# Sliding-window attention beside a long convolution on one core: projections and turns in row halves, bf16 taps through ScalarE, and a new written-out order

## The chip, the cores and the metric

The kernel runs on one core of a Trainium2 chip. Its engines are TensorE (PE: matrix products into PSUM, with weight loads shown as PEld), VectorE (DVE), ScalarE (ACT), GpSimd (POOL), and SyncE (SP), which here only issues DMAs. Each engine works through its own queue in the order in which the program was written for it. The metric is device microseconds of one launch. The kernel before takes 209.3 us (median of 3 runs, 209.15 to 209.7).

## The reference

Two independent parts with S = 2048 rows and D = 576 columns, bf16, written side by side into one output of 2048 x 1152.

```
# part A: attention, 32 heads of 18, each row looks at 8 rows: itself, 2, 4, ... 14 rows back
qkv = x @ wqkv                                   # 2048 x 1728
logits[s, w] = q[s] . k[s - 2w] * 18**-0.5       # masked where s - 2w < 0
a = (softmax(logits) @ v_window) @ wo
# part B: gated long convolution, each of the 576 channels by itself
k_shift[s] = sum over l < 4 of k[s - l] * shift_k[l]
kv = k_shift * v
y = irfft(rfft(kv, 2S) * rfft(ssm_k, 2S))[:S] + kv * ssm_D
out = concat([a, q * y], axis=-1)
```

## The kernel before, in words

Part A. x arrives transposed (channels on partitions), four quarters of 512 rows: three by DMA transposes (`load_x`), the quarter of rows 512 to 1023 by `turn_x`, which loads it straight (`xn`) and turns it on TensorE with 20 identity matmuls (`nx0`, `nx1`, `nx2`; evictions `nx0e` and so on). `heat` gives TensorE 13 matmuls on zeros ahead of that. `project(comp, ct, hh)` computes q, k or v (comp 0, 1, 2) for 128 of the columns (ct 0 to 3; ct 4 is the last 64) and 1024 rows (hh). It sums over 576 = 4 x 128 + 64 channels: four full matmuls for each 512 rows, and one "tail" of 64 channels, which stands in one half of the array's rows. So each q or k unit is eight matmuls of 128x128 and two tails of 64x128; each v unit is sixteen of 128x64 (every ninth column, so that heads land where they are wanted) and four tails of 64x64. ScalarE evicts each unit (`p...e`, L445, L450). `logits` (L473 on VectorE, L481 on TensorE) and `softmax` follow, then `weigh` (L725, L739) and `output` (L790).

Part B. `taps` computes k_shift as matmuls with diagonal 64x64 weights (L535), and VectorE multiplies the PSUM result by v (L543; one of each pair of instructions reads both of its operands backwards, with step -1). `fold` turns kv to rows on partitions and makes sums and differences of mirrored rows, with `F1` = [I, I] and `F2` = [I, -I] (L556, L557, L570, L571). `load_filter` mirrors the filter by a matmul with an exchange matrix `JS`, and a second matmul with `EA` or `EB` adds the one edge row (L605, L606). `filter_spectrum`, `odd_spectrum` and `x_spectrum` are cosine and sine transforms with tables TK and TX, which come from integer multiplications on VectorE (`tab...`, L274, L276) of two iotas that GpSimd writes (`const0`), and ScalarE's Sin. For each of the four output blocks j and three column groups t, `products` (L835) multiplies spectra, `sums` (L859) adds them up in 32x32 matmuls, `inverse` (L892) turns them back, `gate` multiplies by q. In block 3 `carry` adds what block 2 left over, by four identity matmuls of 384 columns for each t (L846), ahead of `sums`; in blocks 1 and 2 a DMA that adds in flight does it (`d{j}{t}`, on GpSimd's queue).

What sets the order: the functions only make a list of named operations. `ORDER`, a table of base-36 numbers, gives the order in which they are written out, and with each a slot: which quarter of PSUM an operation takes, or, for `move`, which engine does it (slot 1 is VectorE, otherwise ScalarE). Within each engine that order is the queue. Names in the texts: `p101` is project(1, 0, 1), `L013` a logits matmul, `a0` to `a3` the weighing matmuls, `Z201` a sum, `i10` an inverse.

`const0` to `const3` fill GpSimd's tables: `const0` the iotas, `const1` the identity, `const3` the head selectors EH (twelve selects) and the pads, `const2` the sign variants of the identity and the 32x32 ones.

## Time and profile before

| | |
|---|---|
| median of 3 runs | 209.3 us (209.15, 209.3, 209.7) |
| span of the profiled execution | 207.9 us (the page gives this span and no time of that execution beside it; the median is 1.4 us above it) |
| busy: PE, DVE, ACT, POOL | 197.1, 177.1, 142.3, 56.9 us |
| TensorE instructions | 3173 matmuls, 3173 weight loads |
| mean DMA rate | 154 GB/s, 32.09 MB |

A row of the groups reads: line, engine, operation, out<-in, shapes, count | busy us of the group, mean ns of one | idle time of the engine ahead of them and who ended it. Busy is the union over the group, so overlapping instructions count once: on TensorE the mean of one is its latency, several run at once, and throughput is read from the starts of the first and the last of a row of them. A stretch of the windows view gives for each engine its busy us there.

### The profile page before, as it was taken

What the parts mean: (1) busy time and instruction counts of PE and PEld (TensorE: products, weight loads), DVE (VectorE), ACT (ScalarE), POOL (GpSimd) and SP (SyncE); (2) the same over time, 40 slices, a digit from 0 to 9 for tenths busy, and PEclk for the clock granted to TensorE, in tenths of its full rate; (3) what the DMA queues carried; (4) which work ended last, traced back from release to release, by engine and by line L of the source; (5) the groups of instructions that cost most, each with busy time, mean ns of one, the idle gap of its engine ahead of it and who ended that gap; (6) DMA issues with size and microseconds to landing.
All of it is one profiled execution on the core that took longest, in us unless ns stands there. A gap on an engine that the chain in (4) does not pass through costs nothing.

```text
span 207.9 us, 7147 instructions
## 1 busy us (share of the span) xinstructions
PE 197.1 (95%) x3173; PEld 133.1 (64%) x3173; DVE 177.1 (85%) x147; ACT 142.3 (68%) x173; POOL 56.9 (27%) x105
## 2 busy tenths in 40 slices
PE   7899999999999999999998969998999999999991
PEld 2433334554644557778787857685689878787690
DVE  7306899769878898889999998999999998999963
ACT  2525479875977715578989857988898767665541
POOL 7981033001041195010899900000003020110000
PEclk9999999999999999999999999999999999999998
DMA  6998979999999959945880263106345865749834
GB/s 170 225 223 150 199 150 194 162 185 130 116 180 213 203 99 188 184 110 120 181 221 6 42 162 103 32 3 199 126 167 114 230 177 141 184 131 255 260 126 114
DMA packets 55254, 32.09 MB, mean 154 GB/s; under 512 B 42032, under 2 KB 52408, under 8 KB 55224
## 3 DMA queue, kind: packets, MB, share of 16 engines
q1 hardware_dynamic: 52520, 26.33, 57.2%
q0 software_dynamic: 2176, 4.73, 13.3%
q10 hardware_dynamic: 528, 0.59, 1.0%
q8 instruction: 24, 0.39, 0.8%
q14 instruction: 6, 0.05, 0.1%
HBM read 5.90 MB, written 4.72 MB: 51 GB/s over the span
## 4 chain that ended last, share of the span: by engine, by line
PE 84%; DMA 5%; ACT 5%; DVE 2%; SPq 1%; issue 1%; DVEq 0%
PE PS L419 24%; PE PS L790 10%; PE PS L892 7%; PE PS L859 6%; PE PS L660 5%; PE PS L481 5%; PE PS L429 4%; PE PS L535 4%; PE PS L645 3%; PE PS L739 3%; ACT mem L745 3%; DMA mem<-in_A_wqkv_dram 3%; DMA mem<-in_A_wo_dram 2%; PE PS L581 2%; PE PS L921 2%; DVE mem L725 2%
## 5 line engine op out<-in xcount | busy, mean ns | idle before, releaser
L419 PE MATMUL PS<-mem 128*64 128x512 bf16 (+1 forms) x304 | 51.5, 385 | 0.7 <-DMA mem<-in_A_wqkv_dram 0.7
L473 DVE TENSOR_TENSOR mem<-mem 128x4096 bf16<-128x4096 bf16 (+1 forms) x20 | 40.7, 2074 | 7.0 <-PE PS L481 4.2
L725 DVE TENSOR_TENSOR mem<-mem 128x4096 bf16<-128x4096 bf16 x18 | 40.3, 2290 | 1.9 <-PE PS L739 1.2
L419 PEld LDWEIGHTS <-mem 128*64 128x64 bf16 (+1 forms) x304 | 26.6, 144 | 22.1 <-issue 6.8
L835 DVE TENSOR_TENSOR mem<-mem 128x4608 bf16<-128x4608 bf16 (+3 forms) x21 | 38.4, 1867 | 1.6 <-PE PS L859 1.4
L190 ACT ACTIVATE mem<-PS 128x768 bf16<-128x768 f32 (+1 forms) x49 | 35.2, 761 | 5.8 <-PE PS L582 2.7
L445 ACT ACTIVATE mem<-PS 128x1024 bf16<-128x1024 f32 x24 | 24.2, 1022 | 19.6 <-PE PS L419 11.8
L193 POOL DMA_DIRECT2D mem<-mem x16 | 13.8, 1009 | 80.9 <-ACT mem L870 45.3
L402 POOL COPY mem<-mem 64x16 bf16<-64x16 bf16 x24 | 18.9, 788 | 22.4 <-ACT mem L445 21.6
L790 PE MATMUL PS<-mem 128*128 128x288 bf16 x160 | 21.9, 286 | 0.9 <-DMA mem<-in_A_wo_dram 0.9
L660 PE MATMUL PS<-mem 128*128 128x192 bf16 x192 | 18.7, 246 | 0.2 <-ACT mem L874 0.2
L790 PEld LDWEIGHTS <-mem 128*128 128x128 bf16 x160 | 15.3, 98 | 5.2 <-DMA mem<-in_A_wo_dram 1.2
L892 PE MATMUL PS<-mem 128*128 128x192 bf16 x192 | 17.7, 246 | 0.1
L660 PEld LDWEIGHTS <-mem 128*128 128x128 bf16 x192 | 15.9, 98 | 1.6 <-issue 1.2
L892 PEld LDWEIGHTS <-mem 128*128 128x128 bf16 x192 | 15.8, 98 | 1.2 <-issue 1.0
L859 PE MATMUL PS<-mem 32*32 32x384 bf16 x960 | 13.9, 325 | 1.3 <-ACT mem L745 0.9
L795 ACT ACTIVATE mem<-PS 128x576 bf16<-128x576 f32 x16 | 10.4, 651 | 5.4 <-PE PS L790 4.5
L543 DVE TENSOR_TENSOR mem<-PS,mem 128x512 bf16<-128x512 f32 (+1 forms) x20 | 11.5, 630 | 2.5 <-PE PS L535 2.4
L859 PEld LDWEIGHTS <-mem 32*32 32x32 bf16 x960 | 9.5, 88 | 5.0 <-issue 2.2
L896 ACT ACTIVATE mem<-PS 128x768 bf16<-128x768 f32 x12 | 9.6, 810 | 4.4 <-PE PS L892 4.4
L870 ACT ACTIVATE mem<-PS 128x1536 bf16<-128x1536 f32 x6 | 8.7, 1451 | 5.4 <-PE PS L859 5.2
L429 PE MATMUL PS<-mem 64*64 64x512 bf16 (+1 forms) x76 | 11.7, 412 | 0.0
(113 smaller groups left out, 285.7 us busy)
## 6 DMA issues: line engine op xcount, KB each, us to landing
mem<-mem SPq DMA_DIRECT2D x16, 256.0 KB, 4.2
mem<-mem POOLq DMA_DIRECT2D x8, 288.0 KB, 5.5
out_dram<-mem SPq DMA_DIRECT2D x16, 144.0 KB, 2.9
mem<-in_B_q_dram SPq DMA_DIRECT2D x4, 576.0 KB, 4.4
mem<-mem SPq DMA_DIRECT2D x6, 384.0 KB, 4.1
mem<-mem POOLq DMA_DIRECT2D x6, 384.0 KB, 4.1
mem<-in_A_wqkv_dram SPq DMA_DIRECT2D x3, 576.0 KB, 5.1
out_dram<-mem SPq DMA_DIRECT2D x6, 288.0 KB, 3.5
```

The lines of the kernel that those rows point to most:

```text
L190: act(o, i, ACT.Copy, scale=scale)
L402: nc.gpsimd.tensor_copy(M1(to, PAD)[64 * a:64 * a + 64], M1(frm, PAD)[64 * a:64 * a + 64])
L419: mm(box.ps[p, jp, :], ws[a % len(ws)], xT(kb, 1024 * hh + 512 * (jp ^ a), 512), start=first and kb == 0, stop=last and kb == 3, tile_posi ...
L429: mm(box.ps[p, jp, :], ws[a % len(ws)][64 * r:64 * r + 64], xT(4, 1024 * hh + 512 * r, 512)[64 * r:64 * r + 64], start=first, stop=not fir ...
L445: op(nm + "e", lambda: act(M(o + pad, [[KH if comp == 2 else 512, 2], [1, 512]]), box.ps, ACT.Copy), box, free=True)
L473: op(f"l{hh}{ug}{ct}", lambda prod=prod, nt=nt, qo=qo, ko=ko, ug=ug: tt(M(prod, [[nt, 4], [1, nt]]), M(qo, [[0, 4], [1, nt]]), M(ko + 2 + ...
L660: mm(box.ps[:, gi // 2, TH * (gi % 2):TH * (gi % 2) + TH], M1(TX + 1024 * c + 512 * pm + 128 * gi, 128), M1(AB + 2304 * i + 1152 * c + 576 ...
L725: op(f"w{n}{ct}", lambda: tt(M(P, [[2048, 2], [256, W], [1, 256]]), M(XB[n], [[2048, 2], [256, W], [1, 256]]), M(vo + 2, [[256, 2], [2, W] ...
L790: mm(box.ps[:, h, 0:HD], M1(lhs, 128), M1(rhs, HD), start=(i == 0), stop=(i == 4))
L835: tt(M(pr + 768 * k, [[2304, n], [768, m], [1, 768]]), M(BS + i * SPB + o + PL * k, [[SPB, n], [PL, m], [1, 768]]), M(VS + (3 - j + i) * S ...
L859: mm(view(box.ps[32 * c:32 * c + 32], box.step * (r // 2) + 512 * (r % 2), [[TH, 2], [1, TH]]), I32S[w][32 * r:32 * r + 32], M(pr + src + ...
L892: mm(box.ps[:, pm, TH * c:TH * c + TH], M1(TI + 512 * sl + 256 * pm + 128 * c, 128), M1((YT if j else YRS[0]) + 1536 * t + 768 * pm + TH * ...
```

## The change

1. `project`: except for q of the first 1024 rows, every 128-channel product is split in two of 64 channels, in the upper and the lower half of the array's rows (`quadrants`). The two halves of the rows work at the same time on different PSUM banks, and in a second phase they swap banks; the tail is a matmul like all others. The operation is in two parts (`p...q`, then `p...`), and between them `between` puts an empty instruction (`p...n`) on the engine that the slot names (0 GpSimd, 1 VectorE, 2 ScalarE, 3 SyncE): it waits for the first part, and the second waits for it. The two 64-column units (ct 4) of q and k, and of v's two halves, become one operation (`project_last`).
2. `fold` turns 64 channels at a time with 64-row weights and 128 moving columns, two at once; each eviction is in two, by ScalarE or VectorE (`move`).
3. `taps`: ScalarE copies PSUM to bf16 (20 copies), VectorE then multiplies SBUF by SBUF (`t...m`).
4. `load_filter`: the second matmul is gone; GpSimd writes the edge row (`hg..`, 1 x 576) after the eviction.
5. Block 3, t 0 and 1: no `carry`; a DMA that adds in flight (`d30`, `d31`) after the eviction, ahead of `inverse`.
6. `gate` of blocks 0 to 2: ScalarE copies the mirrored half out of PSUM (`g..e`), one VectorE multiplication of 1152 columns in place of two of 576 that read PSUM.
7. Weights of q and k arrive in two column parts (256 and 320 columns); `nx0e` to VectorE, `nx2e` to ScalarE.
8. `ORDER` is another table (760 operations in place of 676).

```diff
 ORDER = """
-1o u 26 0 10 20 6 86 8u 1c 90 c 1u 7c 8c 6o 6u 2p 70 2c 96 2u 32 19 36 2i 1i 76 b0 66 3o bx 3u 3c 3i
...
+u 2c 6 o c 0 7o 16 1c 1i 26 1u 1o 12 96 9c 9i 8o 2l 38 2v 4c 20 46 30 3o 3u 3i 40 5u 5o 66 60 7u 3c
...
     def mirrors():
         mirror(M1(JS, 128), 1.0, -128)
-        for t, f in ((EA, float(np.sqrt(0.5))), (EB, 1.0)):
-            nc.gpsimd.memset(M1(t, 128), 0.0)
-            nc.gpsimd.memset(M1(t, 1)[0:1], f)
...
-        dma(f"w{comp}", M(b, [[D, 4], [1, D]]),
-            A_wqkv[0:512, comp * D:(comp + 1) * D].rearrange("(kb p) a -> p kb a", p=128), eng)
+        for c0, c1 in ((0, 256), (256, D)) if comp < 2 else ((0, D),):
+            dma(f"w{comp}" + "b" * (c0 > 0), M(b + c0, [[D, 4], [1, c1 - c0]]),
+                A_wqkv[0:512, comp * D + c0:comp * D + c1].rearrange("(kb p) a -> p kb a", p=128), eng)
...
-            op(f"nx{u}e", (lambda box=box, dst=dst: act(dst, box.ps, ACT.Copy)) if u < 2 else
-               (lambda box=box, dst=dst: nc.vector.tensor_copy(dst, box.ps[:, 0:1, :])), box, free=True)
+            op(f"nx{u}e", lambda box=box, dst=dst, n=len(kbs): move(dst, box.ps[:, 0:n, :]), box, free=True)
...
+    def phase(box, ph, runs):
+        first = None
+        for n in range(max(len(run) for run in runs)):
+            for run in runs:
+                if n < len(run):
+                    o, w, i, pos = run[n]
+                    ins = mm(o, w, i, start=ph == 0 and n == 0, stop=ph == 1 and n == len(run) - 1, tile_position=pos)
+                    first = first or ins
+        if ph:
+            tc.add_manual_dep(first.ins, box.half.ins.name, AFTER, reason="the other half of the rows sums here too")
+        box.half = ins
+
+    def between(nm, box):
+        def fence():
+            nop = (nc.gpsimd, nc.vector, nc.scalar, nc.sync)[Op.slot].nop()
+            tc.add_manual_dep(nop.ins, box.half.ins.name, AFTER, reason="behind the first halves")
+            box.half = nop
+        op(nm + "n", fence, box)
+
+    def quadrants(box, ph, parts):
+        runs = []
+        for lo, cols, r1, x0, bank, tail in parts:
+            r = r1 ^ ph
+            h = slice(64 * r, 64 * r + 64)
+            runs.append([])
+            for kb in [0, 1, 2, 3] + [4] * (tail == r):
+                w = cols(kb)
+                m = w.ap[-1][1]
+                runs[-1].append((box.ps[lo:lo + m, bank, :], w[h], xT(kb, x0, 512)[h], (64 * r, lo)))
+        phase(box, ph, sorted(runs, key=lambda run: run[0][3]))
...
+            op(nm + "q", lambda: quadrants(box, 0, parts), box, 1)
+            between(nm, box)
+            op(nm, lambda: quadrants(box, 1, parts), box)
...
-                op(f"t{pr}{n}{'hl'[lo]}", lambda box=box, s=s, b=b, lo=lo, n=n, nb=nb: tt(
-                    M(KV + 1024 * n + 256 * lo, [[512, nb], [1, 256]]), view(box.ps, b, s), M(VT + 1024 * n + b, s),
-                    ALU.mult), box, free=bool(lo))
+                op(nm, lambda box=box, s=s, b=b, kv=kv: act(kv, view(box.ps, b, s), ACT.Copy), box, free=bool(lo))
+                op(nm + "m", lambda s=s, b=b, n=n, kv=kv: tt(kv, kv, M(VT + 1024 * n + b, s), ALU.mult))
 
     def fold(pr):
+        def turn(box, h, b, mt, to):
+            k = slice(64 * h, 64 * h + 64)
+            o = view(box.ps, 512 * h + to, [[256, 2], [1, 64]])
+            return [(o, w[k], M(ID + i + 64 * h, [[128, 2], [1, 64]])[k], i == 128, h)
+                    for w, i in ((M1(b + 128 * mt, 128), 128), (M1(b + 256 + 128 * mt, 128), 0))]
...
-                    mm(o, M1(JS, 128), M1(a + D * (1 - c) + HD * h, HD), start=True, stop=False)
-                    mm(o, M1(EB if c else EA, 128), M1(a + D * c + HD * h, HD), start=False, stop=True)
+                    mm(o, M1(JS, 128), M1(a + D * (1 - c) + HD * h, HD), start=True, stop=True)
...
+            op(f"hg{d}{c}", lambda c=c: edge(M1(FT + 2 * D * d + D * c, D)[0:1], M1(a + D * c, D)[0:1], c))
...
+            elif j == 3 and first:
+                dma(f"d{j}{t}", M(YT + 1536 * t, [[768, 2], [1, 768]]), M(YRS[2] + 1536 * t + 768, [[-768, 2], [1, 768]]),
+                    nc.gpsimd, accum_op=ALU.add)
...
+            if n == D:
+                op(f"{nm}e{e // w}", lambda box=box, e=e: act(M(y + e, [[D, 2], [1, w]]), box.ps[:, :, 0:w], ACT.Copy), box,
+                   free=True)
...
+        if n == D:
+            op(nm + "l", lambda: tt(M(qb, d), M(y, d), M(qb, d), ALU.mult))
```

Three places where the order moves. The first is GpSimd's queue at the start of the program. Before, the iotas of `const0` (L209 to L212) stand first, then `const1` (L218 to L222), then the twelve selects of `const3`:

```order
L209 IOTA rp_i 128x2
L210 IOTA rp_i 128x2
L212 IOTA mem 128x128 x4
L218 MEMSET mem 128x128
L219 AFFINE_SELECT mem<-mem 128x128 [waits Pool_49]
L222 COPY mem<-mem 64x64 [waits Pool_49]
L222 COPY mem<-mem 64x64
L232 AFFINE_SELECT mem<-mem 128x32 [waits Pool_49]
L234 AFFINE_SELECT mem<-mem 128x32 [waits Pool_49]
```

In the changed kernel the same queue begins with `const1` (L224 to L228) and `const2` (L261 to L268); the selects of `const3` (L237 to L245) follow, and the iotas (L215 to L218) come last, ahead of the two small DMAs of `sh`:

```order
L225 AFFINE_SELECT mem<-mem 128x128 [waits Pool_49]
L228 COPY mem<-mem 64x64 [waits Pool_49]
L228 COPY mem<-mem 64x64
L261 COPY mem<-mem 128x128 [waits Pool_49]
L262 TENSOR_SCALAR mem<-mem 128x128
...
L245 AFFINE_SELECT maskb<-maskb 32x128 [waits Pool_49]
L215 IOTA rp_i 128x2
L216 IOTA rp_i 128x2
L218 IOTA mem 128x128 x4
L199 DMA sh<-in_B_shift_k_dram 128x4
```

The iotas moved from the first place to behind all other constants.

The second is VectorE's queue from the program's start. Before, the table multiplications (L274, L276) wait for GpSimd's iotas, and the eviction of `nx2` (L322) stands behind nine of them:

```order
L334 MEMSET mem 128x256
L207 MEMSET pib 128x1
L213 CAST rp<-rp_i 128x4 [waits Pool_49]
L274 TENSOR_SCALAR mem<-mem,rp 128x512 [waits DVE_49,Pool_49]
L274 TENSOR_SCALAR mem<-mem,rp 128x512 x6
L276 TENSOR_SCALAR mem<-mem 128x1024 [waits DVE_49]
L276 TENSOR_SCALAR mem<-mem 128x1024
L322 CAST mem<-PS 128x512 [waits PE_49]
L350 TENSOR_TENSOR mem<-mem,sh 128x1280 [waits DMASW1_49,DMASW0_49,Pool_49]
```

In the changed kernel L277 and L279 are those multiplications, and L194 is `nx0e`, the eviction of the first two 128-channel groups of the turned x (1024 columns):

```order
L337 MEMSET mem 128x256
L213 MEMSET pib 128x1
L219 CAST rp<-rp_i 128x4 [waits Pool_49]
L277 TENSOR_SCALAR mem<-mem,rp 128x512 [waits DVE_49,Pool_49]
L277 TENSOR_SCALAR mem<-mem,rp 128x512 x2
L279 TENSOR_SCALAR mem<-mem 128x1024 [waits DVE_49]
L277 TENSOR_SCALAR mem<-mem,rp 128x512 x2
L194 TENSOR_SCALAR mem<-PS 128x2x512 [waits PE_49]
```

`nx0e` is new in this queue and stands behind the cast and six table multiplications, of which the first waits for the iotas.

The third is ScalarE's queue around the first taps. Before, two projections' evictions (L445, L450), the tables' evictions (L380), the logits' (L487) and the filters' (L609, L190) follow each other:

```order
L380 ACTIVATE mem<-PS 128x1024 [waits PE_49] x2
L487 ACTIVATE mem<-PS 128x1024 [waits PE_49]
L450 ACTIVATE mem<-PS 128x512 [waits PE_49]
L609 ACTIVATE mem<-PS 128x576 [waits DMAHW0_49,DVE_49,PE_49]
L487 ACTIVATE mem<-PS 128x1024 [waits PE_49]
L609 ACTIVATE mem<-PS 128x576 [waits PE_49] x2
```

In the changed kernel the taps' copies (L583) stand between the same kinds of evictions (L383, L525, L660):

```order
L383 ACTIVATE mem<-PS 128x1024 [waits PE_49]
L525 ACTIVATE mem<-PS 128x1024 [waits PE_49]
L583 ACTIVATE mem<-PS 128x2x256 [waits PE_49]
L583 ACTIVATE mem<-PS 128x2x256
L660 ACTIVATE mem<-PS 128x576 [waits DMAHW0_49,DVE_49,PE_49]
L525 ACTIVATE mem<-PS 128x1024 [waits PE_49]
L583 ACTIVATE mem<-PS 128x256 [waits PE_49]
```

Twenty such copies are added to this queue; those of the first 1024 rows stand ahead of the filters' evictions.

## The prediction

> **What bounds the kernel now.** I read the page's busy times first, then the windows by stretch, then the chain of waits.

> ```profile
> PE 197.1 (95%) x3173; PEld 133.1 (64%) x3173; DVE 177.1 (85%) x147; ACT 142.3 (68%) x173; POOL 56.9 (27%) x105
> ```

> TensorE is busy almost always, VectorE not far behind. The windows say where (columns: stretch, its length, busy us of PE, PEld, DVE, ACT and POOL, granted clock, DMA share, GB/s):

> ```profile
> 8.10:18.70 10.60, 10.60 (x52) 3.97 (x52) 1.50 (x2) 4.77 (x5) 7.71 (x25) 1.00 0.94 204
> 18.70:44.30 25.60, 25.60 (x267) 10.36 (x264) 23.14 (x15) 17.70 (x20) 3.60 (x5) 1.00 0.93 162
> 44.30:77.80 33.50, 33.50 (x324) 18.33 (x324) 28.83 (x26) 22.76 (x28) 10.00 (x12) 1.00 1.08 166
> 77.80:107.90 30.10, 30.10 (x426) 23.21 (x419) 26.75 (x27) 21.66 (x24) 12.78 (x23) 1.00 0.80 167
> 107.90:204.40 96.50, 91.18 (x2097) 74.46 (x2088) 91.15 (x66) 71.69 (x92) 16.29 (x14) 1.00 0.50 138
> 204.40:207.90 3.50, 0.00 (x0) 0.00 (x0) 0.44 (x1) 0.00 (x0) 0.00 (x0) 0.85 0.31 85
> ```

> From 8.1 to 107.9 us TensorE never rests: whatever is taken off it or put ahead of it there moves the end. From 107.9 on, PE and DVE each stand still for some 5.3 of 96.5 us, waiting for each other. So the sum goes by TensorE's path, in three parts: when its projections start, what work is taken off it, and which waits the other engines add once it is shorter.

> **The change part by part.** The start first. Two pieces of the chain, then rows of the timelines of PE and DVE (start, duration):

> ```profile
> 2.78 5.26 DMA mem<-in_A_wqkv_dram
> 8.09 4.49 PE PS L419 x20
> ```

> ```profile
> 1.26 4.02 PE L330 MATMUL PS<-mem 128*128 128x512 bf16 x9 [1.26 <-DVE pib L207]
> 5.08 1.46 PE L316 MATMUL PS<-mem 128*128 128x128 bf16 x20
> 6.38 1.03 PE L330 MATMUL PS<-mem 128*128 128x512 bf16 x4
> ```

> ```profile
> 1.90 2.89 DVE L274 TENSOR_SCALAR mem<-mem,rp 128x512 int32<-128x512 int32 x7 [0.57 <-POOL mem L212]
> 4.83 1.36 DVE L276 TENSOR_SCALAR mem<-mem 128x1024 int32<-128x1024 int32 x2
> 18.70 2.29 DVE L473 TENSOR_TENSOR mem<-mem 128x4096 bf16<-128x4096 bf16 x1 [1.87 <-ACT mem L445]
> ```

> Before, projections start at 8.09. VectorE's table multiplications start at 1.90, 0.03 us behind GpSimd's last iota (0.57 us of waiting are put down to it). In the changed order the iotas stand behind all constants, the tables behind the iotas, `nx0e` behind six tables, and TensorE's first projection reads what `nx0e` writes: every later matmul is queued behind it. How late that is follows from GpSimd's own rows, and a group of VectorE's evictions:

> ```profile
> 0.92 0.12 POOL L209 IOTA rp_i<- 128x2 int32 x1 [0.40 <-POOLq L989]
> 1.08 0.79 POOL L212 IOTA mem<- 128x128 int32 x4
> 1.82 0.20 POOL L218 MEMSET mem<- 128x128 bf16 x1
> 3.38 0.30 POOL L232 TENSOR_SCALAR_AFFINE_SELECT mem<-mem 128x32 bf16<-128x32 bf16 x1
> 6.33 0.21 POOL L234 TENSOR_SCALAR_AFFINE_SELECT mem<-mem 128x32 bf16<-128x32 bf16 x1
> 8.32 0.33 POOL L239 TENSOR_SCALAR_AFFINE_SELECT maskb<-maskb 32x128 bf16<-32x128 bf16 x1
> 12.73 0.29 POOL L258 COPY mem<-mem 128x128 bf16<-128x128 bf16 x1
> 13.92 1.36 POOL L265 TENSOR_SCALAR_AFFINE_SELECT mem<-mem 32x128 bf16<-32x128 bf16 x4
> ```

> ```profile
> L188 DVE TENSOR_SCALAR mem<-PS 128x768 bf16<-128x768 f32 x3 | 2.9, 956 | 0.5 <-PE PS L645 0.5
> ```

> `const1` takes 1.82 to 3.38 = 1.56 us, `const3` 3.38 to 8.65 = 5.27, `const2` 12.73 to 15.28 = 2.55, the iotas 0.92 to 1.87 = 0.95. In a row from 0.92 that ends at 11.25. It may be less: selects took 0.30 beside a busy VectorE and 0.21 once VectorE was done, and VectorE will rest; with eight of them at 0.27 from start to start (2.2 for the 3.2 us from 3.38 to 6.6) and some 0.3 off `const1`, 9.85. I take 10.6, the middle. Then 0.03, five multiplications of 2.89/7 = 0.41 and one of 1.36/2 = 0.68: `nx0e` starts at 13.4. It moves 1024 columns out of PSUM; by 956 ns for 768 that is at most 1.27, I take 1.25: it ends at 14.65. **The projections start 6.55 us later (5.8 to 7.2).** The weights in column parts, meant for an earlier start, are hidden: q's whole weights landed at 8.04 before.

> While it waits, TensorE is idle. The 13 heat matmuls now come first: nine end at 5.08, four more by 5.95, the 20 turns take 1.3 (5.08 to 6.38), so it stops at 7.25 and rests 7.4 us. Its clock then: the last window above shows a mean of 0.85 over 3.5 us without a matmul; if the clock is either full or half, it was half for 1.05 us, so it fell 2.4 us after work ended. And the first nine matmuls of 512 columns took 3.82/9 = 0.42 each, where twenty projections took 4.49/20 = 0.22 each: about 3.8 us at half speed after rest (the granted clock of those 3.8 us isn't in the record; the durations tell). After 7.4 us of rest the first 3.8 us of projections do half the work: **1.9 us lost** (0 if the clock holds, 2.1 if the slow time lasts to 5.45). [...]

> Now the work taken off TensorE, by pieces of the chain and by the first and the last of 16 turns in the timeline:

> ```profile
> 44.57 0.12 PE PS L606
> 44.81 0.12 PE PS L606
> ...
> 79.36 0.21 PE PS L429 x4
> ...
> 97.56 0.42 PE PS L429 x4
> ...
> 185.54 0.65 PE PS L846 x4
> ...
> 190.95 0.65 PE PS L846 x4
> ```

> ```profile
> 93.72 0.27 PE L556 MATMUL PS<-mem 128*128 128x256 bf16 x1
> ...
> 95.36 0.27 PE L557 MATMUL PS<-mem 128*128 128x256 bf16 x1
> ```

> *Projections.* The row halves save no streaming: a unit was eight rounds of 512 columns and a round of tails, and is nine rounds of two or four concurrent matmuls. What goes are changes of the array's shape. The same four tails take 0.21 us behind other 64x64 work and 0.42 with other shapes on both sides: 0.1 per change. Counting shapes along TensorE's queue, there are 100 changes before and 87 in the changed kernel: 13 x 0.1 = 1.3 us (0 to 2.6). The pauses between halves are covered by halves of other units that stand between; the empty instructions on SyncE hold DMAs back that are issued well ahead of need, a gap I price in the rivals. *Filter mirror:* 16 matmuls less; from one L606 to the next pass 0.24 us with one L605 between, so 0.12 each: 1.9 us. The edge copies go to GpSimd, 27% busy. *Turns:* 16 starts from 93.72 to 95.36 give 0.109 each; 72 of them become 72 concurrent pairs of 128 columns. The nearest row is the 20 turns of x, 1.3/20 = 0.065. So 72 x 0.044 = 3.2 us (0 if a pair takes as long as before, 3.8 by 0.056). *Carries:* two of the three, 1.3 us; the DMA in their place is hidden as long as other matmuls stand between eviction and `inverse`:

> ```profile
> mem<-mem POOLq DMA_DIRECT2D x6, 384.0 KB, 4.1
> ```

> Between `d30` and `i30` lie two units of sums, outputs and gates, over 4.1 us; for `i31` it is near, 0 to 0.7 us. **Taken off in all: 1.3 + 1.9 + 3.2 + 1.3 = 7.7 us (3.2 to 9.6).**

> Last, the other engines:

> ```profile
> L543 DVE TENSOR_TENSOR mem<-PS,mem 128x512 bf16<-128x512 f32 (+1 forms) x20 | 11.5, 630 | 2.5 <-PE PS L535 2.4
> ...
> L506 DVE TENSOR_TENSOR mem<-mem 128x512 bf16<-128x512 bf16 x2 | 0.8, 424 | 0.1
> ...
> L766 ACT ACTIVATE mem<-PS 128x512 bf16<-128x512 f32 x2 | 1.2, 598 | 0.0
> ...
> L925 DVE TENSOR_TENSOR mem<-PS,mem 128x576 bf16<-128x576 f32 x6 | 4.5, 754 | 1.2 <-PE PS L921 1.0 <-ACT mem L896 0.2
> ...
> L912 DVE TENSOR_TENSOR mem<-mem 128x1152 bf16<-128x1152 bf16 x3 | 2.2, 749 | 0.0
> ...
> L673 ACT ACT_TABLE_LOAD x1 | 1.3, 1283 | 0.0
> ```

> ScalarE gets 16 copies of 0.6 and four of about 0.4: 11.2 us, most of them between 44 and 108 us. Two copies of 1152 columns and three halves of turns (512 columns) go to VectorE, some -4 by the same rate, and the table load for Exp, written apart from it before, now stands right ahead of the first softmax's Exp, +1.3. So ScalarE has 22.8 + 21.7 + 8.5 = 53 us where TensorE has 63.6 less about 6 = 57.6: 92%, before 70%. VectorE's taps go from 11.5 to 16 x 0.42 + 4 x 0.3 = 8 us if reading backwards keeps the rate of L506, and back to about 10 if those eight stay at the 0.68 of the PSUM form; with the five moves it gets (3 us by L188's rate) it stays near 55: 96%. [...] Where PE and DVE were both at 94% (the window from 107.9) 5.5% of the time was lost to waiting; 5.5% of 57.6 is **3.2 us of new waits** in a stretch that had none (0 to 6). At the end the gates give VectorE back 6 x 0.754 - 3 x 0.749 = 2.3 us, of which I count **0.7** as felt (0 to 2.3), since PE has as little slack there.

> The sum on the profiled execution: 207.9 + 6.55 + 1.9 - 7.7 + 3.2 - 0.7 = 211.15. The median stands 1.4 above that span: **212.5 us.**

> **The rivals.** *The late start is paid back.* New waits are nil, and the new order also halves the 5.3 us that PE loses after 107.9, with all of the 2.3 felt: 207.9 + 6.55 + 1.9 - 7.7 - 2.3 - 2.6 = 203.75, with 1.4 about 205. The place is `z`, `Z` and `i` from 108 on; the kernel is faster from the point at which waits fall by 0.75 us net of new ones. For it: the stretch had slack on both engines. Against it: DVE starts its logits as late as PE, and its own queue is 91 of 96.5 us there. 20%. *ScalarE becomes the bound* between the first taps and the weighing: its evictions free the PSUM that the next projections need, so TensorE waits for each, and SyncE's blocked queue delays k and v of the second half; waits of 7 us instead of 3.2: 216.3. For it: 92% busy in a strict queue with table load and filter copies in it. Against it: half of its work is small. 16%. *The start isn't late:* GpSimd, alone, does the constants in half the time and the clock holds: 6.55 + 1.9 shrink to 2: 206. Against it: its rows, and VectorE waited 8.06 us for the same L265 before `diag`:

> ```profile
> DVE mem L350 <- POOL mem L265: 8.1, 1, 8.1
> ```

> 4%.

> **How the numbers follow.** Forecast 60%, paid back 20%, ScalarE 16%, no late start 4%. A measurement of this kernel tells about 0.3% = 0.6 us from no change, so faster is under 208.7 and slower over 209.9. Faster: 16 of the 20, the 4, and 3 of the forecast's low side (the bounds of the work taken off reach 1.9 lower): 0.23. Same: 4 and 5: 0.09. Slower: 0.68. The range: low side 204.5, just under the paid-back case; high side 218, ScalarE's case with the upper bounds of the start.

> **What would show it.** The first projection (now L450) starts at 14 to 15.5 us, released by VectorE, with the half-speed durations of 0.42 in its first row of matmuls; the first logits start at 27 to 30 instead of 18.7 (10.6 behind the first projection, as before, and the slow clock). The turns' pairs start 0.06 to 0.07 apart. `L583` shows ScalarE over 85% busy around 50 to 110. I am wrong if the projections start by 10 us, if turns take 0.11 a pair, or if PE's idle time between its first projection and its last matmul is under 6 us: it was 5.3, and I expect 8.5.

## The result, and the profile after

The changed kernel takes 225.63 us (median of 4 runs, 224.14 to 230.32) against 209.3: a ratio of 1.0749 (95% interval 1.0687 to 1.0811). The forecast was 212.5, the top of its range 218. Ratios here and below leave out runs over 1.5% above the fastest of the same kernel, while medians hold all runs.

The page of the changed kernel: busy times, the row of the granted clock, and the chain by line.

```profile
PE 194.5 (86%) x3493; PEld 130.4 (58%) x3493; DVE 175.9 (78%) x149; ACT 150.2 (67%) x202; POOL 62.3 (28%) x111
PEclk9958999999999997589999999999999999999998
PE PS L414 17%; DMA mem<-in_B_k_dram 10%; PE PS L843 8%; PE PS L949 6%; PE PS L712 6%; PE PS L913 6%; PE PS L450 4%; PE PS L573 4%; PE PS L792 3%; PE PS L519 2%; PE PS L697 2%; PE PS L627 2%; DMA mem<-in_A_wo_dram 2%; DMA out_dram<-mem 1%; PE PS L978 1%
```

TensorE's share fell from 95% to 86%. The clock falls twice, at the start and in the middle, and a transfer of k, no part of the chain before, is a tenth of it. The windows say where the time is (stretch, length, busy us of PE, PEld, DVE, ACT and POOL, clock, DMA share, GB/s):

```profile
13.70:28.03 14.33, 14.33 (x72) 5.17 (x73) 3.91 (x7) 6.04 (x6) 0.00 (x0) 0.82 1.07 187
28.03:50.83 22.80, 22.80 (x301) 9.73 (x297) 20.95 (x12) 15.59 (x19) 1.84 (x2) 1.00 0.58 111
50.83:82.80 31.97, 29.90 (x444) 15.16 (x444) 30.66 (x28) 24.62 (x35) 19.92 (x21) 1.00 0.91 140
82.80:93.00 10.20, 0.42 (x8) 0.00 (x0) 3.37 (x5) 1.94 (x2) 6.91 (x8) 0.72 1.23 108
93.00:120.80 27.80, 27.68 (x432) 21.69 (x433) 21.07 (x26) 22.60 (x36) 12.62 (x20) 0.92 0.70 139
120.80:222.00 101.20, 93.25 (x2216) 75.77 (x2215) 90.75 (x64) 76.43 (x102) 10.78 (x15) 1.00 0.57 149
```

From 82.8 to 93.0 TensorE stands still and VectorE and ScalarE nearly so, while the DMA engines are full (share 1.23) at a low rate (108 GB/s). TensorE's waits of the whole execution (us, times, longest):

```profile
PE PS L573 <- DMA mem<-in_B_k_dram: 9.8, 1, 9.8
PE PS L450 <- DVE mem L194: 6.3, 1, 6.3
PE PS L913 <- issue: 2.1, 2, 1.4
PE PS L843 <- issue: 1.7, 1, 1.7
PE PS L597 <- ACT mem L660: 1.2, 1, 1.2
PE PS L414 <- SPq L423: 0.9, 1, 0.9
```

L573 is the taps' matmul; the first behind the logits (`t12`) waits for `k1`, a transpose of k that SyncE issues. L450 is the first projection, L423 the empty instruction, L597 the turns. L913 are the small sums (`Z`) and L843 the output products of part A (`o`); "issue" names nobody.

The start, in TensorE's timeline (start, duration):

```profile
1.26 4.94 PE L333 MATMUL PS<-mem 128*128 128x512 bf16 x13 [1.26 <-DVE pib L213]
6.11 1.29 PE L320 MATMUL PS<-mem 128*128 128x128 bf16 x20
13.69 7.05 PE L450 MATMUL PS<-mem 128*128 128x512 bf16 x20 [6.29 <-DVE mem L194]
```

The first projection starts at 13.69, 5.6 us later than before, and twenty of its matmuls take 7.05 us where twenty took 4.49: 2.6 us are lost to the clock. The windows agree: read us by us, the clock is 0.50 from 14 to 18 and 1.00 from 19 on, so its mean of 0.82 over 14.33 us is 5.2 us at half speed, in which 2.6 us of work are lost.

Then SyncE's issue of `k1`, and what the queues moved while it was under way, in 78 to 90 us (packets, MB, share of 16 engines; q1 holds SyncE's transfers, q0 GpSimd's adding ones):

```profile
71.16 7.12 SPq L202 DMA_TRANSPOSE mem<-in_B_k_dram  x1
```

```profile
q1 hardware_dynamic: 1534, 0.39, 76.2%
q0 software_dynamic: 237, 0.48, 52.9%
```

In the chain the transpose takes 21.83 us, from its issue to its landing at 92.99. A packet of q1 took 0.762 x 16 x 12 us / 1534 = 95 ns.

From span to span, 207.9 to 225.3, the loss adds up from these rows and from TensorE's timeline (from the start of one matmul to the start of the next, pauses and slow clock apart):

| | us |
|---|---|
| projections start later | +5.6 |
| slow clock behind that rest | +2.6 |
| `t12` waits for `k1` (82.8 to 93.0) | +10.2 |
| slow clock behind it: `t12`, `t13`, `p200q` 1.71, 1.71, 1.57 in place of 0.86, 0.86, 1.08 | +2.2 |
| `p121` behind its empty instruction on SyncE, the turns `f000` behind the filter's eviction: 1.26 + 1.56, less 0.3 | +2.5 |
| pauses at `Z` and `o` named "issue": 0.96 + 1.77 + 1.97, before 0.67 | +4.0 |
| taken off TensorE: turns 3.5, projections 1.5, taps 1.2, mirror 1.5, carries 1.5 | -9.2 |
| rest | -0.5 |

### The profile page after: what moved, and what is told of

Its sections match the earlier page's. It is cut to its first block, busy times and chain, and to the rows that moved or that the text cites. A ratio compares the mean times of both kernels' runs of the same rounds, so it can differ in the third digit from the quotient of the medians.

```text
span 225.3 us, 7854 instructions
## 1 busy us (share of the span) xinstructions
PE 194.5 (86%) x3493; PEld 130.4 (58%) x3493; DVE 175.9 (78%) x149; ACT 150.2 (67%) x202; POOL 62.3 (28%) x111
## 4 chain that ended last, share of the span: by engine, by line
PE 67%; DMA 13%; POOL 5%; ACT 4%; issue 4%; DVE 3%; SPq 1%; DVEq 0%; POOLq 0%; ACTq 0%
PE PS L414 17%; DMA mem<-in_B_k_dram 10%; PE PS L843 8%; PE PS L949 6%; PE PS L712 6%; PE PS L913 6%; PE PS L450 4%; PE PS L573 4%; PE PS L792 3%; PE PS L519 2%; PE PS L697 2%; PE PS L627 2%; DMA mem<-in_A_wo_dram 2%; DMA out_dram<-mem 1%; PE PS L978 1%
## 5 line engine op out<-in xcount | busy, mean ns | idle before, releaser
L414 PE MATMUL PS<-mem 64*64 64x512 bf16 (+1 forms) x612 | 51.8, 387 | 0.9 <-SPq L423 0.9
L196 ACT ACTIVATE mem<-PS 128x768 bf16<-128x768 f32 (+3 forms) x64 | 43.4, 749 | 7.9 <-PE PS L320 4.6
L414 PEld LDWEIGHTS <-mem 64*64 64x64 bf16 (+1 forms) x612 | 28.3, 147 | 21.3 <-issue 5.8
L199 POOL DMA_DIRECT2D mem<-mem x18 | 16.0, 955 | 83.9 <-ACT mem L924 66.8
L843 PE MATMUL PS<-mem 128*128 128x288 bf16 x160 | 21.9, 286 | 1.8 <-issue 1.7
L573 PE MATMUL PS<-mem 64*64 64x512 bf16 x144 | 11.7, 434 | 9.8 <-DMA mem<-in_B_k_dram 9.8
L843 PEld LDWEIGHTS <-mem 128*128 128x128 bf16 x160 | 15.1, 98 | 6.6 <-issue 3.2
L405 POOL COPY mem<-mem 64x16 bf16<-64x16 bf16 x24 | 13.9, 577 | 15.8 <-PE PS L414 12.8
L583 ACT ACTIVATE mem<-PS 128x512 bf16<-128x512 f32 (+1 forms) x20 | 9.9, 558 | 12.4 <-PE PS L573 12.4
L913 PE MATMUL PS<-mem 32*32 32x384 bf16 x960 | 14.3, 325 | 2.3 <-issue 2.1
L848 ACT ACTIVATE mem<-PS 128x576 bf16<-128x576 f32 x16 | 10.4, 654 | 8.8 <-PE PS L843 6.5
L584 DVE TENSOR_TENSOR mem<-mem 128x512 bf16<-128x512 bf16 (+1 forms) x20 | 7.5, 417 | 10.5 <-ACT mem L583 10.3
L450 PE MATMUL PS<-mem 128*128 128x512 bf16 x32 | 10.2, 476 | 6.3 <-DVE mem L194 6.3
L573 PEld LDWEIGHTS <-mem 64*64 64x64 bf16 x144 | 5.0, 119 | 15.0 <-DMA mem<-in_B_k_dram 10.3
## 6 DMA issues: line engine op xcount, KB each, us to landing
mem<-mem POOLq DMA_DIRECT2D x8, 384.0 KB, 5.0
mem<-mem SPq DMA_DIRECT2D x6, 384.0 KB, 4.2
```

The lines of the kernel that those rows point to most:

```text
L196: act(o, i, ACT.Copy, scale=scale)
L414: ins = mm(o, w, i, start=ph == 0 and n == 0, stop=ph == 1 and n == len(run) - 1, tile_position=pos)
L450: mm(box.ps[:, jp, :], wcol(comp, kb, ct)[0], xT(kb, t0 + 512 * jp, 512), start=kb == 0, stop=False)
L573: mm(box.ps[64 * c:64 * c + 64, bank, :], dg(w, h, l), kt(w, h, ab, l), start=(l == 0), stop=(l == 3), tile_position=(64 * h, 64 * c))
L843: mm(box.ps[:, h, 0:HD], M1(lhs, 128), M1(rhs, HD), start=(i == 0), stop=(i == 4))
L913: mm(view(box.ps[32 * c:32 * c + 32], box.step * (r // 2) + 512 * (r % 2), [[TH, 2], [1, TH]]), I32S[w][32 * r:32 * r + 32], M(pr + src + ...
```

## The experiments

**The start and k's transpose.** My theory: two places of the order make most of the loss, the iotas behind all constants, and `k1` so late on SyncE that GpSimd's adding DMAs run beside it. The rival: whatever is mended there is waited for elsewhere. Order edits of the changed kernel, the three together:

```
 GpSimd:  - const1 const2 const3 const0      + const0 const1 const2 const3
 SyncE:   - kt1 p121n ... va1 hc0 vb1 k1     + kt1 k1 p121n ... va1 hc0 vb1
```

The iotas alone:

> Edit: in the order alone, const0 (the iotas) goes ahead of const1, as in the kernel before; nothing else moves. Theory A (two mishaps of the order, the start and k's second transpose, make up the loss): the first projection starts near 8.0 us in place of 13.7 and without the slow clock (-2.3), so the first logits start near 20; the wait for k at t12 stays, since its transpose still runs beside the adding DMAs: 225.6 - 5.6 - 2.3 = about 217.5. Rival B (three engines that are nearly full lose the time wherever it is gained): the gain at the start is mostly given back before the weighing, 222 or more.

Measured: 217.17 (ratio to before 1.0341, 1.0289 to 1.0393), 8.5 us gained, as the theory had it. The first projection starts at 8.70, and the wait for k is still there:

```profile
PE PS L573 <- DMA mem<-in_B_k_dram: 6.9, 1, 6.9
```

`nx0e` on ScalarE in place of VectorE, the iotas left last:

> Edit: slot of nx0e alone, so that ScalarE and not VectorE evicts it; the iotas stay last on GpSimd. If the late start comes from nx0e being queued behind the tables on VectorE, the first projection starts near 9.5 us (ScalarE does nx1e, nx2e, nx0e one after the other from 7.2) although the tables are as late as before, the clock does not fall, and the end moves by some -5 to -6.5: 219 to 221. If it were anything else that waits for GpSimd, the start stays near 13.7.

Measured: 220.49, one run, with the first projection at 9.76. Either edit mends the start, since it is their combination (the tables wait for the iotas, and `nx0e` stands behind the tables) that delayed it. `k1` alone, then with the iotas:

> Edit: in the order alone, the DMA k1 is issued right behind kt1, 12 us earlier, ahead of the filters' adding DMAs. Theory A: k lands before t12 needs it (by 72), the 10 us wait of TensorE and VectorE and the slow clock behind it (about 1.7 us on t12, t13 and p200q) go: 225.6 - 10 - 2 = about 213.5. Rival B: the wait moves to another DMA of the same full queues (v's second half, the adds): 220 or more.

> Edit: both of the moves, the iotas first and k1 behind kt1. Theory A: the two gains add up, 225.6 - 8 - 12 = about 205.5, faster than the kernel before (209.3): the parts of the change other than these two places of the order are then worth about -4. Rival B: 214 or more, since ScalarE and VectorE are as full as TensorE.

Measured: 227.28 (1.0865, 1.0796 to 1.0934) and 220.39 (1.0448, 1.0348 to 1.0548). The rival's times held, though at a place that neither expectation named. The wait for k is gone, but now the empty instruction of `p121` stands on SyncE behind the issue of both transposes. The `k1` version's SyncE, and TensorE's wait for it:

```profile
58.33 6.22 SPq L202 DMA_TRANSPOSE mem<-in_B_k_dram  x2
```

```profile
PE PS L414 <- SPq L423: 9.5, 2, 5.9
```

An issue that takes 6 us may be no matter for the DMAs behind it, but it is one for an instruction on TensorE's path in the same queue. Two further edits tell the collision from the lateness: all adding DMAs moved behind `t10`, `k1` left where it is; and iotas first with `k1` one place further back (`kt1 p121n k1`).

> The changed kernel with one thing moved: all adding DMAs that GpSimd issues for the filter's halves (eight of 288 KB between 70 and 88 us) come behind the first shape-changing product of that stretch, so that none of them is in flight while k's second transpose, which SyncE still issues at 71 us, is moving. Theory A (the adding DMAs slow the transpose's 256-byte packets from 20 to 48-108 ns, and that is why it lands at 93 us): it lands at 80 to 84 us, TensorE's wait ahead of t12 falls from 10.4 us to under 2, the second fall of the clock goes with it, and the time is 212 to 216. Rival B (SyncE issues the transpose too late, whoever shares the engines with it): it still lands past 90 us, and the time stays 223 to 227.

> The changed kernel with const0 ahead of const1 on GpSimd and with k's second transpose issued on SyncE right behind the empty instruction of p121n, instead of ahead of it. Theory A (the transpose was issued late into the adding DMAs, and in the version before this one the only harm was that p121n's empty instruction stood behind its 6 us of issuing): the wait ahead of t12 is under 1 us and that ahead of p121 under 2 us; the version with const0 first alone was 217.2, its wait of 7.5 us and some 2 us of slow clock go, and the time is 206 to 210. Rival B (every place on SyncE hits another empty instruction, because SyncE is full there): a wait of 4 to 7 us comes up at another product, p231, p200 or p201, and the time stays 213 to 219.

The first, one run: 226.01, but the wait for k is gone, with the transpose issued at the same 71.1 us. q1 from 72 to 78 us, with no adding DMA beside it:

```profile
q1 hardware_dynamic: 4900, 1.24, 103.1%
```

That is 1.031 x 16 x 6 / 4900 = 20 ns a packet in place of 95. With the adding DMAs out of the way the transpose is fast, though issued as late, so they are part of the cause. That some fly beside it is not enough, however. In the changed kernel from 72 to 78 us, with the first three adds issued, and in the kernel before from 60 to 66 us, with two beside this same transpose, the queues moved:

```profile
q1 hardware_dynamic: 3365, 0.85, 77.8%
q0 software_dynamic: 159, 0.33, 42.0%
```

```profile
q1 hardware_dynamic: 2789, 0.70, 99.4%
q0 software_dynamic: 146, 0.29, 26.5%
```

By the same working that is 22 and 34 ns a packet. What made it 95 from 78 us on was not shown. The time that the edit freed went into the next waits: TensorE waits 6.6 us more behind SyncE than in the changed kernel (6.0 at once, a projection of v whose empty instruction stands behind the spreads in the queue) and 2.2 us more at the pauses named "issue". The spreads (`s000` and so on) are DMAs that copy the softmax weights to where the weighing products read them. The second: 213.76 (1.0187, 1.0136 to 1.0238), `k1` waited for no more. Of the 16 us lost, 12 are these two places of the order. But the start is now 0.2 us earlier than before and TensorE has 9.2 us less to do, so some 14 us of waits remained to be found.

**The empty instructions.** In that version (213.8) TensorE waits 4.3 us for `p201`'s empty instruction on SyncE, behind four issues of spreads that take 11 us, and VectorE 4.9 us for the spreads themselves. TensorE's wait, SyncE's row and VectorE's row:

```profile
PE PS L414 <- SPq L423: 5.2, 2, 4.3
```

```profile
80.46 11.14 SPq L199 DMA_DIRECT2D mem<-mem  x4
```

```profile
95.33 4.49 DVE L778 TENSOR_TENSOR mem<-mem 128x4096 bf16<-128x4096 bf16 x2 [4.93 <-DMA mem<-mem]
```

Three versions of it move empty instructions: six of SyncE to ScalarE and VectorE; then, from the same base, GpSimd's of `p221` and `p210` to ScalarE; then these with `p201n` on ScalarE, `kt1` behind `p121n`, and the first two adding DMAs right behind their inputs.

> The same as the version with const0 first and k's second transpose behind p121n, and with the six empty instructions of SyncE (p001n, p121n, p231n, p200n, p201n, p24n) on ScalarE and VectorE instead. Theory A (TensorE's waits of 1.3 us at p021q and of up to 4.6 us ahead of p201 are empty instructions that stand behind DMA issues of SyncE): these waits go, and it is 2 to 5 us below its neighbour with the empty instructions on SyncE, 203 to 207. Rival B (ScalarE is what comes last there, and an empty instruction on it waits as long): within 1 us of its neighbour.

> The version with const0 first and k's second transpose behind p121n (213.8 us), with GpSimd's empty instructions of p221 and p210 on ScalarE instead. Theory A (GpSimd, in order, stands 7 us behind p221's empty instruction, so its adding DMAs start at 62.6 and run into the spreads of the weights, whose issues take 11 us there instead of 4): the adds start by 58, the spreads' issues take under 7 us, VectorE's wait of 4.9 us ahead of the first weighing product falls under 2, and the time is 209 to 212. Rival B (ScalarE's queue delays the empty instructions more than GpSimd did, or the adds wait for the filter's halves anyway): 213 to 216.

> The same with three more places of the order changed: p201's empty instruction on ScalarE, k's first transpose behind p121n too, and the first two adding DMAs right behind their inputs. Theory A (all that is left of the loss up to the first weighing product is queues on SyncE and GpSimd): TensorE's waits at p021q (1.1) and ahead of p201 (4.5) go, the first weighing product starts by 92 instead of 95.3, and the time is 206.5 to 209. Rival B (a queue freed at one place comes back as a wait at another): 211 to 215.

Measured: 214.41 (1.0133, 1.0079 to 1.0186), 215.13 (1.0263, 1.0221 to 1.0305) and 214.76 (1.0257, 1.0203 to 1.0311). The rivals held: the time was not saved. In the last, TensorE waits for VectorE's weighing products in place of SyncE:

```profile
PE PS L792 <- DVE mem L778: 4.4, 1, 4.4
```

In the last two the last six adding DMAs are still issued at 77 to 85 us, behind the last edge copies (L643), and the spreads' issues still take 11.5 and 12.3 us. That the adds slow the spreads too was not shown.

**Parts undone.** From the 213.8 version, the gate back on VectorE straight from PSUM (`g..l` on VectorE in the place of `g..e`), and the taps likewise:

```diff
-                op(nm, lambda box=box, s=s, b=b, kv=kv: act(kv, view(box.ps, b, s), ACT.Copy), box, free=bool(lo))
-                op(nm + "m", lambda s=s, b=b, n=n, kv=kv: tt(kv, kv, M(VT + 1024 * n + b, s), ALU.mult))
+                op(f"t{pr}{n}{'hl'[lo]}", lambda box=box, s=s, b=b, kv=kv, n=n: tt(
+                    kv, view(box.ps, b, s), M(VT + 1024 * n + b, s), ALU.mult), box, free=bool(lo))
```

> The version with const0 first and k's second transpose behind p121n (213.8 us), with one part undone: the mirrored gate by VectorE straight from PSUM, without ScalarE's copies. Theory A (VectorE, in order, stands behind ScalarE's copies for up to 4.8 us at a gate, and TensorE waits for VectorE then): 210.5 to 212.5. Rival B (the gate's 2.3 us of VectorE's time are worth more than that wait): 214 to 216. If neither: within 0.6 us.

> The same version (213.8 us) with another part undone: the taps by VectorE straight from PSUM, without ScalarE's 20 copies. Theory A (the 11 us of copies on ScalarE delay the evictions for which TensorE waits between 44 and 110 us, 5 to 8 us of waits there): 209.5 to 212.5. Rival B (VectorE, with 4 us more, is what is waited for): 215 to 218.

Measured: 218.53 (1.0466, 1.0384 to 1.0548) and 224.47 (1.0732, 1.0663 to 1.0801). Both theories fell, and the rivals were too small. In this order ScalarE's copies save time; without them VectorE is what TensorE waits for in the taps' version:

```profile
PE PS L518 <- DVE mem L510: 4.0, 3, 1.8
PE PS L413 <- POOLq L422: 3.2, 1, 3.2
PE PS L655 <- DVE mem L581: 3.1, 2, 2.8
```

**Parts alone in the kernel before.** If what comes off TensorE moves the end, the pairs of turns put into the kernel before (`fold` of the change, its second eviction on ScalarE behind the first) must be worth 3.8 us. A second version adds the mirror of the change and the first of its carries:

> The kernel before with one part of the change alone: the 72 turns as concurrent pairs of 64 rows, with two evictions on ScalarE where there was one; order, taps, projections and carries are those of before. Theory A (what the change takes off TensorE between 8 and 108 us reaches the end as long as nothing new is waited for): 16 turns took 1.75 us before and 0.9 in pairs, so 3.8 us come off and the time is 204.8 to 206.5. Rival B (the stretch from 108 on, where TensorE and VectorE wait for each other, gives it back): 208 to 209.5.

> The kernel before with three parts: the turns in pairs, the filter's mirror without edge matmuls (copies of one row on GpSimd instead) and the first of the three carries by DMA. Theory A: 3.8 + 1.9 + 0.65 us come off TensorE and the time is 202.5 to 204.5. Rival B (given back from 108 us on, or GpSimd's row copies hold back its adding DMAs): 206.5 to 209.5.

Measured: 212.78 (209.21 to 214.06 in ten runs; 1.006, 1.0013 to 1.0106), and with mirror and one carry 212.46 (1.0109, 1.0036 to 1.0182). Nothing was gained, a little lost. My theory was then that VectorE's weighing products, back to back from 95 us on, took the gain. A version that leaves out a quarter of them, and so computes another output, without the pairs and with them:

```diff
-        Ps = [product(n, ct) for ct in range(4)]
+        Ps = [product(n, ct) for ct in range(3)]
+        Ps.append(Ps[2])
```

> The kernel before with a quarter of VectorE's weighing products left out (four of sixteen multiplications of 4096 columns, 2.24 us each; the weighing reads the third product twice, so the output is another). TensorE's work and the order are untouched. Theory A (from 95 us on VectorE's products, back to back, set the end, and not TensorE, though its busy share is the higher one on the page): VectorE has 9 us less to do and the time falls to 201 to 206. Rival B (TensorE sets the end there): within 1 us of 209.4.

> The same, with the turns in pairs besides. With all products the pairs gained nothing (209.2 to 212.0 in undisturbed runs). Theory A (VectorE's products took the gain back): now that VectorE has 9 us less in that stretch, the pairs are worth 2 to 4 us, and the time is that much below the version without them, 198 to 203. Rival B (something else takes it back: the extra evictions on ScalarE, or the clock): no more than 1 us below it.

Measured: 209.66 (1.0007, 0.9992 to 1.0021) and 211.43 (1.0077, 1.0048 to 1.0106). The theory fell: 9 us off VectorE are worth nothing, with the pairs or without. The timeline shows another loss. TensorE in the version with pairs and fewer products:

```profile
194.33 2.80 PE L900 MATMUL PS<-mem 128*128 128x192 bf16 x32 [1.95 <-ACT mem L878]
200.25 0.71 PE L867 MATMUL PS<-mem 32*32 32x384 bf16 x36 [1.24 <-issue]
```

The products of `inverse` (L900, `i22`) waited for no ScalarE copy before. Counted from 0 at the program's first, with weight loads and waits, the instruction behind this pause is TensorE's number 6081, and that behind the second 6337: 23 x 256 + 193 and 24 x 256 + 193. In the kernel before the pause of 0.67 us stands at 5825, 22 x 256 + 193; in the changed kernel the pauses of 0.96, 1.77 and 1.97 us stand at 5313, 6337 and 6593, again all 193 past a multiple of 256 (these times are from one start to the next; the rows give the idle part of them). Each ends 1.3 to 1.6 us behind the landing of a 16 KB packet of the queue of instructions (q8). That such a packet holds 256 of TensorE's instructions fits their number: 2 x 3173 and 2 x 3493 matmuls and weight loads make 24 and 27 whole blocks of 256, and q8 brought, before and after:

```profile
q8 instruction: 24, 0.39, 0.8%
```

```profile
q8 instruction: 27, 0.44, 0.9%
```

The changed kernel's last two pauses:

```profile
205.72 0.35 PE L913 MATMUL PS<-mem 32*32 32x384 bf16 x7
207.52 1.63 PE L913 MATMUL PS<-mem 32*32 32x384 bf16 x121 [1.44 <-issue]
209.09 1.03 PE L843 MATMUL PS<-mem 128*128 128x288 bf16 x7
211.80 0.54 PE L843 MATMUL PS<-mem 128*128 128x288 bf16 x3 [1.69 <-issue]
```

**The boundary of the block.** The new theory: 128 small sums with their weight loads are 256 instructions in 1.7 us; when they run, the next block is late, and how late hangs on where the boundary falls among the slow instructions between the groups. It can be moved without changing the work, by small matmuls in TensorE's idle start:

```diff
+            for k in range(56 if n == 4 else 0):
+                r = slice(32 * (k % 4), 32 * (k % 4) + 32)
+                mm(box.ps[r, 1, 0:16], M1(PR, 32)[r], M1(PR, 16)[r], start=True, stop=True,
+                   tile_position=(32 * (k % 4), 32 * (k % 4)))
```

> The kernel before with the turns in pairs (212.8 us median, 209.2 to 214), and 56 matmuls of 32x32 on 16 columns more in the idle start of TensorE, whose result nobody reads: 112 instructions, which with the 144 of the pairs make 256. Nothing else is changed. Theory F (TensorE's instructions come by DMA in blocks of 256; where 256 of them run in under 4 us, as in the three groups of 128 sums at the end, the next block is late and TensorE stands still; the pairs moved the boundary into the last instructions of such a group): the pause of 2.2 us at i22 and the slow clock behind it go back to the 0.7 us of the kernel before, and the time is 206.5 to 208.5. Rival G (the pause is the wait for ScalarE's copy that the profile names, or the gain is lost elsewhere): 209 to 213 as without them.

> The kernel before, with 64 such matmuls in TensorE's idle start and no other change: half a block. Theory F: the boundary falls right behind the group Z310 to Z313, a pause of 2 us comes up at i22 or close to it where the kernel before had 0.7 us ahead of Z312, and with the slow clock that may follow the time is 210.5 to 213. Rival G (the place in the block doesn't matter): 209 to 209.8.

> The version with const0 first and k's second transpose behind p121n (213.8 us), with 70 such matmuls more and two of the heating ones less: 136 instructions. Theory F: the boundary goes from the first third of the sums Z310 and from g20f0 to the last third of each group, the pauses of 2.2, 1.4 and 0.5 us shrink to under 1 us in all, and the time is 209.5 to 211.5. Rival G: 212.5 to 215, as without them.

The pairs with the boundary where it was before: **208.27 us, 0.995 of the kernel before (0.9931 to 0.997)**, the only version here that beats it. The kernel before with the boundary half a block away: **212.73, 1.0159 (1.0123 to 1.0195)**, with no other change. TensorE in the first and in the second, at the same `i22` and the sums ahead of it:

```profile
190.10 1.11 PE L871 MATMUL PS<-mem 32*32 32x384 bf16 x73
191.37 0.90 PE L871 MATMUL PS<-mem 32*32 32x384 bf16 x55 [0.16 <-issue]
192.20 3.09 PE L904 MATMUL PS<-mem 128*128 128x192 bf16 x32
```

```profile
195.01 0.83 PE L896 MATMUL PS<-mem 128*128 128x192 bf16 x8
198.16 2.14 PE L896 MATMUL PS<-mem 128*128 128x192 bf16 x24 [2.31 <-issue]
```

The second stops ahead of its instruction 6081, where the theory put the pause, and the profile says "issue" where it named ScalarE above. Of the 3.4 us between the spans 2.2 lie at this pause and 0.6 at the start, where a weight came late. The idle matmuls themselves don't explain it: 56 of them went with a faster kernel and 64 with a slower one. The 4 us in the first of the three expectations were an estimate, and no run shows such a bound: the changed kernel's last pause stands behind a block that ran in 2.6 us (from 207.52), the second pause of the version with pairs and fewer products behind one that ran in 4.7 us (from 194.33 to 199.01). In the 213.8 version the shift missed: 215.36 (1.0213, 1.0171 to 1.0255). Its three pauses (0.5, 2.2, 1.4 us) became one of 2.1 in place of the under 1 us expected, so the theory tells where a pause can stand, but did not tell here how long it is. `inverse` then waited for the DMA that replaced a carry (L953), which the pauses had probably covered, and a projection of v waited 3.3 us behind SyncE:

```profile
PE PS L418 <- SPq L427: 4.2, 2, 3.3
PE PS L953 <- DMA mem<-mem: 3.0, 1, 3.0
```

## Why the prediction was wrong, step by step

*The start: right in kind,* a little under its bounds. Forecast 6.55 later (5.8 to 7.2), 14.65; it was 5.6, 13.69. GpSimd did its constants faster than the rows beside a busy VectorE had it: the iotas began at 8.6 and ended at 9.5, not 10.6. *The slow clock: right in kind,* 2.6 for 1.9; the matmuls ran at half speed for some 5.2 us. The prediction took 3.8 from the first heat matmuls of before. In the window view the clock is 0.53 from 12.00 to 13.69, so it was at half for 1.6 us ahead of the projections and for 1.6 + 5.2 = 6.8 us in all; what sets that length was not shown.

*Work taken off: right, and too small.* 9.2 for 7.7. The turns' pairs start 0.053 us apart (16 instructions in 0.62 us from the first start to the last end, one 0.22 long: (0.62 - 0.22)/15 x 2; forecast 0.065), the projections saved 1.5 for 1.3, and TensorE's part of the taps, which the prediction left as it was, 1.2. On VectorE the taps take 7.5 us for 8 forecast. The half of them that read one operand backwards take as long as the others, 409 to 424 ns for 512 columns but for the first, 875; the forward row L506 had 424. The mean below holds 512 and 256 columns:

```profile
L583 ACT ACTIVATE mem<-PS 128x512 bf16<-128x512 f32 (+1 forms) x20 | 9.9, 558 | 12.4 <-PE PS L573 12.4
L584 DVE TENSOR_TENSOR mem<-mem 128x512 bf16<-128x512 bf16 (+1 forms) x20 | 7.5, 417 | 10.5 <-ACT mem L583 10.3 <-issue 0.2
```

*The gates:* 0.7 was counted; undoing them cost 4.8 us in the 213.8 version, part of it in pauses at L843, so their own size stays open.

*New waits: the step that failed.* 3.2 us were taken from the shares of ScalarE and VectorE; it was 10.2 + 2.2 + 2.5 + 4.0 = 18.9, and ahead of 110 us ScalarE is named for only 1.2 of it. The sentence that carried the error is that "the empty instructions on SyncE hold DMAs back that are issued well ahead of need". No empty instruction held `k1` itself: between `kt1` and `k1` stands only that of `p121`, done at 60.3. What failed is "well ahead of need". I took the need from before, where `k1`'s place in SyncE's queue and the adding DMAs' in GpSimd's were others: before, this transpose was issued at 61.0, with two adds beside it, and nobody waited for it; now it is issued at 71.2, and the first of eight adds of 288 KB in the same microsecond. Of a DMA moved in the order I priced neither the place of issue nor what flies beside it. Nor did I price what an empty instruction pays for standing behind an issue, which the `k1` version shows at 5.9 us. The rival that named SyncE's blocked queue put it at 7 us of waits in all, under ScalarE's name.

*"Whatever is taken off it moves the end": too simple.* VectorE was not the bound, as the version with a quarter of the products left out shows; but 3.8 us less of TensorE's work gained nothing until its instruction blocks were back in place, and then 1.1 us of median and 1.6 of span. Where the other 2 us went stays open.

*The rivals.* Paid back: no, the last stretch went from 96.5 to 101.2 us. ScalarE the bound: its share was 77% and 81% in the stretches from 50.8 and from 93.0 us (24.62 of 31.97, 22.60 of 27.80), where over 85% was to show it, and the runs with its copies undone are slower. A start that isn't late: no.

*Open:* what keeps the 213.8 version 4.4 us above the kernel before. Its rows name 4.1 us of pauses at the blocks, 4.3 behind the spreads' issues and, behind that wait, a clock of 0.58 over the 6.09 us from 94.78, which is some 2.6 us more; each attempt on one of them brought up another.

## What to carry to other kernels

A DMA that is moved has to be priced by what flies beside it at its new place and by every instruction queued behind its issue, above all an instruction on the path of another engine. Work that comes off a busy engine counts only if its next waits are named too: DMA landings, clock and instruction blocks included. Before believing a difference of 1 to 2% in a kernel with dense stretches of small instructions, count where the engine's pauses stand in its instruction stream, and shift the stream once with idle work to see what the place alone is worth.

## What the runs showed of the hardware

A transpose DMA that ran at 20 ns a packet with no adding DMA beside it took 95 ns a packet over 12 us beside several of them, and 21.8 us to land; in the 6 us ahead of that it ran at 22 ns, with adds beside it too. Its issue held SyncE for up to 7.1 us, four spreads together up to 12.3 us.

The profile put one such pause (1.95 us, L900 behind L878) down to a ScalarE copy that had nothing to do with it. The place in the instruction stream told them apart, not the name.
